# A feed-forward output layer with its weights stationary, 512 tokens moving, and results turned by VectorE

## The chip, the cores and the metric

The kernel runs on one core of one Trainium2 chip. The metric is the device time of one execution in microseconds, from the first to the last instruction with what the launch adds; the median of three runs counts. TensorE (PE in the profile) multiplies a stationary 128x128 operand, loaded by a weight load (PEld), with a moving operand of up to 512 columns and writes to PSUM, eight banks of 128 x 512 words. VectorE (DVE), ScalarE (ACT) and GpSimd (POOL) do the elementwise work, and SyncE (SP) issues nearly all DMAs.

## The reference

Three parts follow one another: a gated linear attention, a soft mixture of experts, and a feed-forward layer. The change is in the last; the weights of the second part's outputs (`c`) are built next to it.

```python
# x: 3072 tokens x 384 (batch 4, 768 each), 8 experts with 4 slots = 32 slots
logits = x @ phi                                   # 3072 x 32
d = softmax of logits over the tokens;  slot_input = d.T @ x
slot_out[e] = np.maximum(slot_input[e] @ w1[e], 0.0) @ w2[e]      # 32 x 384
c = softmax of logits over the slots               # 3072 x 32
x = c @ slot_out
# feed-forward: w_in 384 x 2048, w_out 2048 x 384
h = x @ w_in
g = np.maximum(0.01 * h, h)
return g @ w_out
```

## The kernel before, in words

All instructions are recorded with a cost and their dependences in a planner (class `Plan`), which sets the order on each engine by due times (`backward`, `forward`) and then emits the program. The code's order is thus only a wish; `plan.lead` makes operations due earlier. Buffers come from tags (`Tag`), each with a number of rotating buffers, and a buffer is taken in the order of the code: `t_w` has 33, `t_wi` 8, `t_x` and `t_q` and `t_qt` 5, `t_sc` and `t_yt` 4, `t_kt` and `t_cs` 2.

The program has three stages. **Attention** (0 to about 238 us) works on 12 units of 128 tokens; the last lines of a unit that matter here are the masking pass on VectorE (line 671), which the product of line 693 waits for. **Experts** (about 245 to 276 us) is a stream of 64 slabs of 384 KB of expert weights, loaded by SyncE as buffers come free; line 944 is the first expert layer, line 980 the second. The product of `slot_out` with `w_in` (lines 1024 to 1039) is made once, into `gs`, so that the first layer of the feed-forward part multiplies the weights `c` (32 slots, split in a high and a low part: 128 rows) with `gs`. **Feed-forward** (276 us to the end) is the stage of the change.

There, tokens are taken in `NB` = 8 blocks of `NG` = 384. `combine` makes the softmax over slots, for 18 of the 24 token tiles in one go ahead of the last attention unit's end and for the other six later. `combine_t` splits a block's weights in a high part (GpSimd, line 886) and a low part (VectorE, line 887), turns them on TensorE (line 891) and evicts them on ScalarE (line 894) to `cT[j]`. Six of the eight blocks are turned there, through the attention's PSUM bank `btr`, and the last two in the middle of the feed-forward stage.

`ffn1(j, f)` makes 128 of the 2048 hidden rows for block `j`: one matmul with 384 moving columns (line 1049), leaky ReLU on ScalarE (line 1051), rounded high part on ScalarE (line 1052), remainder on VectorE (line 1053). `ffn2(j, t, f)` adds 128 hidden rows into the result of token tile `t` of the block: the hidden values are stationary (128 hidden x 128 tokens) and the weights `woh`, `wol` (high and low part, 384 columns) move; three matmuls (lines 1066 to 1068) per step. After the 16th step ScalarE evicts the tile (line 1075) and SyncE stores it in rows of 1536 bytes (line 1076). Two blocks run side by side while the output weights are still converted (`conv_wo`: lines 445 to 449, 477 and 478); the other six follow one by one. The last block goes tile by tile.

## Time and profile before

| | us |
|---|---|
| median of three runs | 503.58 (503.57 to 504.87) |
| profiled execution, span | 503.0 |
| PE busy / DVE busy / ACT busy | 485.6 / 324.2 / 358.9 |
| 0 to 232 us: PE, DVE, ACT busy, DMA share | 219.69, 209.82, 211.45, 0.63 |
| 232 to 276 us | 42.45, 20.72, 13.87, 0.98 |
| 276 to 499.6 us | 223.50, 93.70, 133.15, 0.09 |
| 499.6 to 503 us | 0.00, 0.00, 0.48, 0.40 |

The profiled execution's span lies 0.6 us under the median of the runs. Busy times of engines overlap one another, and a matmul's printed length overlaps the next matmul's: what one costs in a row of matmuls is the distance between starts. A share is read stage by stage, since different engines and the DMA take turns in setting the pace.

### The profile page before, as it was taken

The numbers are of one execution on the slowest core, as the hardware profiler recorded it, in microseconds if no ns is written. First come the engines' busy times: TensorE is split into PE (matmuls) and PEld (weight loads), VectorE is DVE, ScalarE is ACT, GpSimd is POOL, SyncE is SP. The second block draws the span as 40 slices with busy tenths as digits, with TensorE's granted clock in tenths as the row PEclk, the third lists the DMA queues.
The fourth block names the chain that finished last, engine by engine and source line by source line (L and its number), as shares of the span: only waits on it lengthen the run. The fifth ranks groups of instructions, "written<-read, shape, count | busy, mean of one in ns | idle before, by whom it ended". The sixth has DMA issues, their size and how long they took to land.

```text
span 503.0 us, 10542 instructions
## 1 busy us (share of the span) xinstructions
PE 485.6 (97%) x4091; PEld 444.1 (88%) x4091; DVE 324.2 (64%) x686; ACT 358.9 (71%) x684; POOL 17.6 (3%) x37
## 2 busy tenths in 40 slices
PE   8797989999999999999999999999999999999997
PEld 8685879889989989888645999999999999999996
DVE  3778799999999999996544999324500552035300
ACT  6998999999999998955315999069801993079602
POOL 1010000001000100001000000000000000000000
PEclk9998999999999999999999999999999999999999
DMA  8877072473656596689999221011000010010002
GB/s 296 327 162 232 3 222 65 128 192 69 193 151 190 131 273 201 211 296 336 302 398 395 76 63 33 0 48 48 1 1 31 17 48 1 1 47 18 32 1 94
DMA packets 46890, 67.09 MB, mean 133 GB/s; under 512 B 22004, under 2 KB 28132, under 8 KB 46840
## 3 DMA queue, kind: packets, MB, share of 16 engines
q1 hardware_dynamic: 46088, 65.99, 41.1%
q8 instruction: 32, 0.52, 0.4%
q10 hardware_dynamic: 432, 0.39, 0.3%
q0 software_dynamic: 320, 0.03, 0.1%
q14 instruction: 18, 0.15, 0.1%
HBM read 61.59 MB, written 4.81 MB: 132 GB/s over the span
## 4 chain that ended last, share of the span: by engine, by line
PE 69%; ACT 14%; DVE 8%; DMA 7%; issue 1%; SPq 1%; DVEq 0%; ACTq 0%
PE b L1066 13%; PE b L1068 13%; PE b L1067 13%; PE bm L693 5%; PE bsc L668 5%; PE btr L653 4%; PE b L1049 4%; DMA w<-in_w_dram 4%; PE bc L571 3%; PE bsc L710 3%; ACT L186 3%; ACT qt L659 2%; DMA S<-in_w_dram 1%; DVE sc L671 1%; DMA w<-in_a_dram 1%
## 5 line engine op out<-in xcount | busy, mean ns | idle before, releaser
L1053 DVE TENSOR_TENSOR w<-x,w 128x384 fp32r<-128x384 f32 x128 | 69.0, 555 | 104.6 <-ACT w L1052 103.8
L1066 PE MATMUL b<-w 128*128 128x384 f32 x384 | 128.5, 335 | 0.0
L1068 PE MATMUL b<-w 128*128 128x384 f32 x384 | 128.3, 334 | 0.0
L1067 PE MATMUL b<-w 128*128 128x384 f32 x384 | 128.3, 334 | 0.0
L1066 PEld LDWEIGHTS b<-w 128*128 128x128 f32 x384 | 72.1, 188 | 0.3 <-ACT x L1051 0.2
L1067 PEld LDWEIGHTS b<-w 128*128 128x128 f32 x384 | 72.1, 188 | 0.0
L1068 PEld LDWEIGHTS b<-w 128*128 128x128 f32 x384 | 72.1, 188 | 0.0
L1075 ACT ACTIVATE k<-b 128x384 f32<-128x384 f32 x24 | 11.4, 488 | 79.1 <-PE b L1068 78.9
L1052 ACT ACTIVATE w<-x 128x384 fp32r<-128x384 f32 x128 | 63.5, 525 | 4.9 <-PE b L1068 3.2
L1051 ACT ACTIVATE x<-b 128x384 f32<-128x384 f32 x128 | 59.9, 487 | 2.5 <-PE b L1049 1.6
L668 PE MATMUL bsc<-qt,kt 96*128 96x128 f32 x384 | 51.1, 278 | 0.3 <-DVE kt L657 0.2
L668 PEld LDWEIGHTS bsc<-qt,kt 96*128 96x128 f32 x384 | 46.6, 192 | 1.9 <-DVE kt L657 0.5
L693 PE MATMUL bm<-sc,w 128*64 128x128 f32 (+1 forms) x384 | 35.5, 274 | 0.0
L671 DVE TENSOR_TENSOR sc<-bsc,tri_r 128x512 f32<-128x512 f32 x48 | 32.3, 683 | 3.1 <-PE bsc L668 2.7
L186 ACT ACT_TABLE_LOAD x25 | 32.1, 1283 | 2.6 <-issue 2.2
L653 PE MATMUL btr<-ident,q 128*96 128x128 f32 x192 | 30.0, 279 | 2.6 <-ACT qt L659 1.9
L693 PE MATMUL bm<-qt,S 96*48 96x128 f32 x320 | 31.1, 271 | 0.0
L653 PE MATMUL btr<-ident,k 128*96 128x128 f32 x192 | 29.6, 278 | 1.5 <-ACT kt L659 0.7
L710 PE MATMUL bsc<-w,k 128*96 128x48 f32 x320 | 29.8, 246 | 0.5 <-DVE sc L671 0.5
L710 PEld LDWEIGHTS bsc<-w,k 128*96 128x96 f32 x320 | 29.0, 165 | 1.1 <-DVE sc L671 0.7
L653 PEld LDWEIGHTS btr<-ident,q 128*96 128x96 f32 x192 | 20.9, 129 | 9.3 <-ACT qt L659 3.9
L659 ACT ACTIVATE qt<-btr 96x512 f32<-96x512 f32 x48 | 28.1, 589 | 1.1 <-PE btr L653 0.7
(183 smaller groups left out, 814.1 us busy)
## 6 DMA issues: line engine op xcount, KB each, us to landing
w<-in_w_dram SPq DMA_DIRECT2D x50, 384.0 KB
w<-in_qkv_dram SPq DMA_DIRECT2D x36, 384.0 KB
w<-in_a_dram SPq DMA_DIRECT2D x22, 384.0 KB
w<-in_wi_dram SPq DMA_DIRECT2D x16, 384.0 KB
w<-in_wo_dram SPq DMA_DIRECT2D x16, 384.0 KB
out_dram<-k SPq DMA_DIRECT2D x24, 192.0 KB
cs<-in_w_dram SPq DMA_DIRECT2D x4, 384.0 KB
k<-in_w_dram SPq DMA_DIRECT2D x6, 192.0 KB
```

Of the source, the lines that this page charges most:

```text
L186: self.preload(TABLES[name])
L653: T.transpose(b()[:96, P * i:P * i + P], src()[:, i].rearrange("p t d -> p (t d)"), ident)
L659: act(512, lambda b=b, t=t: A.activation(t()[:96], b()[:96, :].rearrange("p (i t) -> p i t", t=P), AF.Copy), [b], [t])
L668: T.matmul(b()[:, P * i:P * i + P], lhsT=k()[:96, i, :], rhs=q()[:96, i, :], start=True, stop=True)
L693: T.matmul(y()[64 * j:64 * j + m, o:o + P], lhsT=l, rhs=r, start=kind == 0, stop=kind == 1 or c == 0)
L710: T.matmul(b()[:96, D * i:D * i + D], lhsT=ks[i // 4]()[:, i % 4].rearrange("p t d -> p (t d)"), rhs=v()[:, D * g:D * g + D], start=True, ...
L1051: act(NG, lambda: A.activation(u(), b()[:, :NG], AF.Prelu, alpha=0.01), [b], [u])
L1052: act(NG, lambda: A.activation(g()[:, 0], u(), AF.Copy), [u], [(g, 0)])
L1053: dve(c_dve(NG), lambda: V.tensor_tensor(g()[:, 1], u(), g()[:, 0].bitcast(F32), op=ALU.subtract), [u, (g, 0)], [(g, 1)])
L1066: T.matmul(b()[:, :DM], lhsT=lh, rhs=wh()[:, i], start=f == FO[0], stop=False)
L1067: T.matmul(b()[:, :DM], lhsT=ll, rhs=wh()[:, i], start=False, stop=False)
L1068: T.matmul(b()[:, :DM], lhsT=lh, rhs=wl()[:, i], start=False, stop=f == FO[-1])
```

## The change

The block size `NG` goes from 384 to 512 tokens, so there are six blocks. A block is now 128 tokens of each of the four batch rows.

- `ffn2` of the first five blocks swaps the operands: the weights are stationary (every third column of `woh` or `wol`, a step of three words, for output columns 3m + k), and 512 tokens move. Three results per block (`k` = 0 to 2), each with 16 x 3 matmuls. A result has output columns on its partitions and tokens along its columns; VectorE turns it in blocks of 32 x 32 on the way out of PSUM, with a step of three words in the destination, into `of[j]` (tag `cs`). When all three are there, SyncE stores 16 pieces of 32 partitions x 4 x 96 words, rows of 384 bytes.
- the last block (`ffn2_last`) keeps the old form, 4 tiles with 384 columns of weights moving; its four tiles go step by step together, two are evicted by ScalarE and two by VectorE. It is held behind the last `ffn2` of the block before.
- `ffn1` works on 512 columns, with its high part in a `wi` buffer, the low part in a `w` buffer and the value before in an `sc` buffer.
- `combine` makes the softmax for 20 tiles in one go and for the last four later. `combine_t` is called block by block: two blocks after the expert layers are recorded, the third in the middle of the first two blocks, and each later one in the middle of the block before. It no longer uses the attention's PSUM bank.

```diff
--- before.py
+++ after.py
@@ -28,7 +28,7 @@
 G = 2 * H
 W = G * D
...
-NG = 3 * P
+NG = 4 * P
 NB = NT // NG
 NFC = DFF // P
 RND = 1.5 * 2.0 ** 23
@@ -860,38 +860,36 @@
 
     cT = {}
 
-    def combine(j0, j1, bank, after):
-
...
+        lgs = [("lg", c) for c in range(j0, j1)]
+        n = 4 * (j1 - j0) * NSL
+        t0 = slice(4 * j0, 4 * j1)
+        bc = lambda: rm()[:, t0].unsqueeze(2).to_broadcast([P, 4 * (j1 - j0), NSL])
+        key = (rm, j0)
+        lk = [("cw", j) for j in range(j0, j1)]
         dve(c_dve(n), lambda: V.tensor_reduce(rm()[:, t0], logits[:, t0], axis=AX.X, op=ALU.max), lgs, [key], after=after)
...
-        if j0 == 0:
-            combine_t(j0, j1, bank, lk)
-
-    def combine_t(j0, j1, bank, lk):
-        for j in range(j0, j1):
-            c4, b, t = (t_k if 4 <= j < 6 else t_kt)([P, 3, 4, NSL], F32R), bank(), slice(3 * j, 3 * j + 3)
-            ct = cT[j] = (t_q, t_yt)[j // 5]([P, NG], F32R)
-            w = lambda t=t: logits[:, t].unsqueeze(2).to_broadcast([P, 3, 2, NSL])
-            pool(c_pts(192), lambda c4=c4, w=w: GP.tensor_scalar(c4()[:, :, 0:2, :], w(), 1.0, 0.0, op0=ALU.mult, op1=ALU.add), [lk], [(c4, 0)])
-            dve(c_dve(192), lambda c4=c4, w=w: V.tensor_tensor(c4()[:, :, 2:4, :], w(), c4()[:, :, 0:2, :].bitcast(F32), op=ALU.subtract), [(c4, 0), lk], [(c4, 1)])
-
...
-            pe(0.33, tr, [(c4, 0), (c4, 1)], [b], after=[phi_mm] if 4 <= j < 6 else [])
-            act(384, lambda ct=ct, b=b: A.activation(ct(), b()[:, :NG], AF.Copy), [b], [ct])
+        dve(c_dve(n), lambda: V.tensor_tensor(logits[:, t0], logits[:, t0], bc(), op=ALU.mult), [key], lk)
+
+    def combine_t(j):
+        c4, b, t = t_kt([P, 4, 4, NSL], F32R), bank(), slice(4 * j, 4 * j + 4)
+        ct = cT[j] = (t_yt if j < 4 else t_qt if j < 5 else t_kt)([P, NG], F32R)
+        w = lambda: logits[:, t].unsqueeze(2).to_broadcast([P, 4, 2, NSL])
+        lk = ("cw", j)
+        pool(c_pts(256), lambda: GP.tensor_scalar(c4()[:, :, 0:2, :], w(), 1.0, 0.0, op0=ALU.mult, op1=ALU.add), [lk], [(c4, 0)])
+        dve(c_dve(256), lambda: V.tensor_tensor(c4()[:, :, 2:4, :], w(), c4()[:, :, 0:2, :].bitcast(F32), op=ALU.subtract), [(c4, 0), lk], [(c4, 1)])
+
+        def tr():
+            for k in range(4):
+                T.transpose(b()[:, P * k:P * k + P], c4()[:, k].bitcast(F32).rearrange("p r s -> p (r s)"), ident)
+
+        pe(0.44, tr, [(c4, 0), (c4, 1)], [b])
+        act(NG, lambda: A.activation(ct(), b()[:, :NG], AF.Copy), [b], [ct])
 
 
     psb = Area(tc, "psb", after=(psa,), space=PSUM)
@@ -900,7 +898,7 @@
     t_rm = Tag(mem, "rm", [P, NTILE], 1)
     rm = t_rm()
     plan.lead = 30.0
-    combine(0, 6, b_tr, ())
+    combine(0, NB - 1, ())
     plan.lead = 0.0
     rd, siT, wb = t_sm([P, 1]), t_dd([P, 3, NSL]), t_kt([P, 4, NSL])
     dg, mt = t_kt([P, P]), t_sm()
@@ -1046,33 +1044,67 @@
     def ffn1(j, f):
         b = bank()
         w, o = gs[f // 4], P * (f % 4)
-        pe(0.17, lambda: T.matmul(b()[:, :NG], lhsT=w()[:, o:o + P], rhs=cT[j](), start=True, stop=True), [(w, o // 256), cT[j]], [b])
-        u, g = t_x(), t_w([P, 2, NG], F32R)
+        pe(0.227, lambda: T.matmul(b()[:, :NG], lhsT=w()[:, o:o + P], rhs=cT[j](), start=True, stop=True), [(w, o // 256), cT[j]], [b])
+        u, gh, gl = t_sc(), t_wi([P, NG], F32R), t_w([P, NG], F32R)
         act(NG, lambda: A.activation(u(), b()[:, :NG], AF.Prelu, alpha=0.01), [b], [u])
-        act(NG, lambda: A.activation(g()[:, 0], u(), AF.Copy), [u], [(g, 0)])
-        dve(c_dve(NG), lambda: V.tensor_tensor(g()[:, 1], u(), g()[:, 0].bitcast(F32), op=ALU.subtract), [u, (g, 0)], [(g, 1)])
-        hl[j, f] = g
-
-    ob = {}
-
-    def ffn2(j, t, f):
+        act(NG, lambda: A.activation(gh(), u(), AF.Copy), [u], [gh])
+        dve(c_dve(NG), lambda: V.tensor_tensor(gl(), u(), gh().bitcast(F32), op=ALU.subtract), [u, gh], [gl])
+        hl[j, f] = gh, gl
+
+    ob, of, outs = {}, {}, []
+
+    def ffn2(j, k, f):
+
+        if f == FO[0]:
+            ob[j, k] = bank()
+            if k == 0:
+                of[j] = t_cs([P, NG // 32, 32, 3])
+        b, (gh, gl), o = ob[j, k], hl[j, f], of[j]
+        wh, wl, i = woh[f // 2], wol[f // 2], f % 2
+
+        def mmul():
+            h, l = (w()[:, i].rearrange("p (m k) -> p m k", k=3)[:, :, k] for w in (wh, wl))
+            T.matmul(b()[:, :NG], lhsT=h, rhs=gh(), start=f == FO[0], stop=False)
+            T.matmul(b()[:, :NG], lhsT=h, rhs=gl(), start=False, stop=False)
+            T.matmul(b()[:, :NG], lhsT=l, rhs=gh(), start=False, stop=f == FO[-1])
+
+        op = pe(0.68, mmul, [gh, gl, (wh, i), (wl, i)], [b])
+        if f == FO[-1]:
+            outs.append(op)
+            dve(c_dve(NG) + 0.1, lambda: V.transpose(o()[:, :, :, k], b()[:, :NG].rearrange("p (n t) -> p n t", t=32)), [b], [(o, k)])
+            if k == 2:
+                for a in range(4):
+                    for bi in range(B):
+                        r0 = S * bi + P * j
+
+                        def store(a=a, bi=bi, r0=r0):
+                            SY.dma_start(
+                                out[r0:r0 + P, 96 * a:96 * a + 96].rearrange("(n t) d -> t n d", t=32),
+                                o()[32 * a:32 * a + 32, 4 * bi:4 * bi + 4].rearrange("p n d k -> p n (d k)"),
+                            )
+
+                        plan.add("SP", 0, store, [(o, k) for k in range(3)], [], nbytes=P * 96 * 4)
+
+    def ffn2_last(j, t, f):
         if f == FO[0]:
             ob[j, t] = bank()
-        b, g = ob[j, t], hl[j, f]
+        b, (gh, gl) = ob[j, t], hl[j, f]
         wh, wl, i = woh[f // 2], wol[f // 2], f % 2
 
         def mmul():
-            lh, ll = g()[:, 0, P * t:P * t + P], g()[:, 1, P * t:P * t + P]
+            lh, ll = gh()[:, P * t:P * t + P], gl()[:, P * t:P * t + P]
             T.matmul(b()[:, :DM], lhsT=lh, rhs=wh()[:, i], start=f == FO[0], stop=False)
             T.matmul(b()[:, :DM], lhsT=ll, rhs=wh()[:, i], start=False, stop=False)
             T.matmul(b()[:, :DM], lhsT=lh, rhs=wl()[:, i], start=False, stop=f == FO[-1])
 
-        pe(0.515, mmul, [(g, 0), (g, 1), (wh, i), (wl, i)], [b])
+        pe(0.52, mmul, [gh, gl, (wh, i), (wl, i)], [b], after=[outs[-1]])
         if f == FO[-1]:
             o = t_k()
-            c, bi = divmod(3 * j + t, B)
-            r0 = S * bi + P * c
-            act(384, lambda: A.activation(o(), b()[:, :DM], AF.Copy), [b], [o])
+            r0 = S * t + P * j
+            if t % 2:
+                act(384, lambda: A.activation(o(), b()[:, :DM], AF.Copy), [b], [o])
+            else:
+                dve(c_dve(384), lambda: V.tensor_copy(o(), b()[:, :DM]), [b], [o])
             plan.add("SP", 0, lambda: SY.dma_start(out[r0:r0 + P, :], o()), [o], [], nbytes=P * DM * 4)
 
     load_slabs(LATE[0])
@@ -1092,7 +1124,9 @@
     layer2(1)
     output(0)
     output(1)
-    combine(6, NB, bank, [si])
+    combine(NB - 1, NB, [si])
+    combine_t(0)
+    combine_t(1)
     plan.lead = 25.0
     product()
     for f in FO[:4]:
@@ -1110,19 +1144,21 @@
             if i + ahead < NFC:
                 ffn1(j, FO[i + ahead])
         for j in range(2):
-            for t in range(3):
-                ffn2(j, t, f)
+            for k in range(3):
+                ffn2(j, k, f)
+        if i == NFC // 2:
+            combine_t(2)
     for j in range(2, NB):
-        if j == 3:
-            combine_t(6, NB, bank, ("cw", 6))
-        for f in FO:
+        for i, f in enumerate(FO):
             ffn1(j, f)
             if j < NB - 1:
-                for t in range(3):
-                    ffn2(j, t, f)
-    for t in range(3):
-        for f in FO:
-            ffn2(NB - 1, t, f)
+                for k in range(3):
+                    ffn2(j, k, f)
+            else:
+                for t in range(B):
+                    ffn2_last(j, t, f)
+            if i == NFC // 2 and j < NB - 1:
+                combine_t(j + 1)
     plan.emit()
     for a in (mem, psb, dram):
         a.close()
```

The order that the planner makes of it, at the places that the steps of the prediction rest on. First VectorE at the end of attention, before: `logits` and `rm` are the softmax over slots, `sc<-bsc,tri_r` is the masking pass.

```order
L671 TENSOR_TENSOR sc<-bsc,tri_r 128x512
L875 TENSOR_SCALAR rm<-rm 128x18
L876 RECIPROCAL rm<-rm 128x18
L877 TENSOR_TENSOR logits<-logits,rm 128x576
L671 TENSOR_TENSOR sc<-bsc,tri_r 128x512
L887 TENSOR_TENSOR k<-logits,k 128x3x64 x2
L887 TENSOR_TENSOR kt<-logits,kt 128x3x64
L448 SCALAR_TENSOR_TENSOR w<-w 128x384
L657 COPY kt<-btr 96x512
L671 TENSOR_TENSOR sc<-bsc,tri_r 128x512
L449 SCALAR_TENSOR_TENSOR wi<-w 128x384
L887 TENSOR_TENSOR kt<-logits,kt 128x3x64
```

After, up to the last masking pass and the reduction that follows it:

```order
L449 SCALAR_TENSOR_TENSOR wi<-w 128x384
L671 TENSOR_TENSOR sc<-bsc,tri_r 128x512
L874 TENSOR_REDUCE rm<-logits 128x20
L657 COPY kt<-btr 96x512
L671 TENSOR_TENSOR sc<-bsc,tri_r 128x512
L875 TENSOR_SCALAR rm<-rm 128x20
L876 RECIPROCAL rm<-rm 128x20
L877 TENSOR_TENSOR logits<-logits,rm 128x640
L671 TENSOR_TENSOR sc<-bsc,tri_r 128x512
L759 TENSOR_REDUCE mx<-bsc 128x1
```

The subtractions of line 887 are no longer among the masking passes; the softmax passes are 640 wide instead of 576.

Second, TensorE in the middle of a block, before. The first name behind the arrow is the moving operand, the second the stationary one; numbers tell buffers apart.

```order
L1049 MATMUL b_4922<-q_3438,qt_3922 128x384
L1066 MATMUL b_4814<-w_4060,w_4850 128x384
L1067 MATMUL b_4814<-w_4060,w_4850 128x384
L1068 MATMUL b_4814<-w_4070,w_4850 128x384
L1066 MATMUL b_4821<-w_4060,w_4850 128x384
L1067 MATMUL b_4821<-w_4060,w_4850 128x384
L1068 MATMUL b_4821<-w_4070,w_4850 128x384
```

After, in the fourth block:

```order
L1047 MATMUL b_5021<-yt_4676,qt_3884 128x512
L1067 MATMUL b_4879<-wi_5006,w_4201 128x512
L1068 MATMUL b_4879<-w_5011,w_4201 128x512
L1069 MATMUL b_4879<-wi_5006,w_4213 128x512
L1067 MATMUL b_4885<-wi_5006,w_4201 128x512
L1068 MATMUL b_4885<-w_5011,w_4201 128x512
L1069 MATMUL b_4885<-wi_5006,w_4213 128x512
```

Per 128 hidden rows of a block it is ten matmuls as before (a third group of three isn't shown), each 512 wide, for 512 tokens instead of 384; the hidden values (`wi`, `w`) now move and the output weights stand.

Third, TensorE where the second and third block meet, after. `b_3944` and its two neighbours are results of the first block, `b_3952`, `b_3967` and `b_3980` of the second, `b_4545` of the third.

```order
L1069 MATMUL b_3944<-wi_4509,w_4400 128x512
L1047 MATMUL b_4601<-yt_4270,qt_3878 128x512
L1067 MATMUL b_3952<-wi_4522,w_4393 128x512
L1068 MATMUL b_3952<-w_4527,w_4393 128x512
L1069 MATMUL b_3952<-wi_4522,w_4400 128x512
L1047 MATMUL b_4609<-yt_4270,qt_3888 128x512
L1047 MATMUL b_4616<-yt_4270,qt_3884 128x512
L1047 MATMUL b_4618<-yt_4270,qt_3888 128x512
L1067 MATMUL b_3967<-wi_4522,w_4393 128x512
L1068 MATMUL b_3967<-w_4527,w_4393 128x512
L1069 MATMUL b_3967<-wi_4522,w_4400 128x512
L1047 MATMUL b_4631<-yt_4270,qt_3884 128x512
```

The first-layer matmuls of the third block stand in a bunch between the second block's last groups, and the last group of `b_3980` stands far later, among the fourth block's last.

## Rows read from the trace of the kernel before

**Rows 1.** Busy us (instructions) by stretch: PE, PEld, DVE, ACT, POOL; PEclk, DMA, GB/s
```profile
232.00:252.00 20.00, 19.38 (x275) 14.47 (x275) 10.44 (x40) 6.57 (x18) 1.00 (x3) 1.00 0.92 311
252.00:272.00 20.00, 19.07 (x232) 8.70 (x228) 6.34 (x33) 4.17 (x8) 0.99 (x2) 1.00 1.03 400
...
280.00:499.00 219.00, 219.00 (x1268) 218.89 (x1267) 89.96 (x187) 129.24 (x298) 0.00 (x0) 1.00 0.09 28
```

**Rows 2.** Timeline of TensorE, output layer: start, length, line, operation, operands, count
```profile
329.79 0.33 PE L1066 MATMUL b<-w 128*128 128x384 f32 x1
...
330.83 0.33 PE L1066 MATMUL b<-w 128*128 128x384 f32 x1
```

**Rows 3.** Timeline, matmuls of 256 columns of lines 1032 and 1033, and what follows
```profile
275.78 0.28 PE L1032 MATMUL b<-w,sc 128*128 128x256 f32 x1
...
276.73 1.04 PE L1049 MATMUL b<-q,qt 128*128 128x384 f32 x5
```

**Rows 4.** Timeline, line 571: 512 and 256 columns in turn; merged lengths
```profile
121.95 0.74 PE L571 MATMUL bc<-w,tri_r 128*128 128x512 f32 x3
...
122.18 0.52 PE L571 MATMUL bc<-w,tri_r 128*128 128x256 f32 x2
...
122.30 0.40 PE L571 MATMUL bc<-w,tri_r 128*128 128x512 f32 x1
```

**Rows 5.** Groups by line and form: operands, count, busy us, mean ns, idle before
```profile
L448 DVE SCALAR_TENSOR_TENSOR w<-w 128x384 int32<-128x384 int32 x32 | 17.3, 550 | 0.1
...
L478 DVE TENSOR_TENSOR w<-w 128x384 fp32r<-128x384 f32 x16 | 8.8, 552 | 0.1
```

**Rows 6.** Timeline of TensorE, weight loads of 128 columns with 32 columns moving
```profile
243.37 0.93 PE L923 MATMUL bm<-kt,acc 128*128 128x32 f32 x6
244.13 0.42 PE L832 MATMUL bc<-ident 128*128 128x128 f32 x2
```

**Rows 7.** Timeline of VectorE at the end of attention
```profile
224.86 0.75 DVE L872 TENSOR_TENSOR logits<-logits,rm 128x576 f32<-128x576 f32 x1
...
229.73 0.92 DVE L887 TENSOR_TENSOR k<-logits,k 128x192 fp32r<-128x192 f32 x2
...
230.84 0.55 DVE L448 SCALAR_TENSOR_TENSOR w<-w 128x384 int32<-128x384 int32 x1
...
232.97 0.34 DVE L887 TENSOR_TENSOR kt<-logits,kt 128x192 fp32r<-128x192 f32 x1
233.24 0.68 DVE L671 TENSOR_TENSOR sc<-bsc,tri_r 128x512 f32<-128x512 f32 x1
```

**Rows 8.** Timeline of TensorE between the last attention product and the expert layer
```profile
237.51 0.87 PE L891 MATMUL btr<-ident,kt 128*128 128x128 f32 x6
238.22 0.55 PE L735 MATMUL bm<-ident,yt 112*128 112x112 f32 x4
...
244.85 1.50 PE L944 MATMUL b<-w,dd 128*32 128x256 f32 x24 [0.30 <-DVE dd L925]
```

**Rows 9.** The chain of work that ended last: start, length, what
```profile
260.67 7.81 DMA w<-in_w_dram
268.52 1.49 PE b L980 x10
```

**Rows 10.** Timeline of VectorE at the start of the feed-forward stage
```profile
277.06 0.56 DVE L1053 TENSOR_TENSOR w<-x,w 128x384 fp32r<-128x384 f32 x1
```

**Rows 11.** Groups of the whole program, columns as in rows 5
```profile
L1052 ACT ACTIVATE w<-x 128x384 fp32r<-128x384 f32 x128 | 63.5, 525 | 4.9 <-PE b L1068 3.2
L1051 ACT ACTIVATE x<-b 128x384 f32<-128x384 f32 x128 | 59.9, 487 | 2.5 <-PE b L1049 1.6
...
L659 ACT ACTIVATE qt<-btr 96x512 f32<-96x512 f32 x48 | 28.1, 589 | 1.1 <-PE btr L653 0.7
```

**Rows 12.** Timeline at the end of the program
```profile
499.59 0.49 ACT L1075 ACTIVATE k<-b 128x384 f32<-128x384 f32 x1 [0.60 <-PE b L1068]
500.11 0.33 SPq L1076 DMA_DIRECT2D out_dram<-k  x1
```

More of the change, by code (lines that the diff above doesn't have):

```diff
@@ L861, in tile_kernel, with combine @@
     cT = {}
-    def combine(j0, j1, bank, after):
-        i0, i1 = 3 * j0, 3 * j1
-        lgs = [("lg", c) for c in range(i0 // 4, (i1 + 3) // 4)]
-        n = (i1 - i0) * NSL
-        t0 = slice(i0, i1)
-        bc = lambda: rm()[:, t0].unsqueeze(2).to_broadcast([P, i1 - i0, NSL])
-        key, lk = (rm, j0), ("cw", j0)
+    def combine(j0, j1, after):
+        lgs = [("lg", c) for c in range(j0, j1)]
[4 more added lines that the diff above has]
+        lk = [("cw", j) for j in range(j0, j1)]
@@ L871, in combine @@
         dve(c_dve(n), lambda: V.tensor_reduce(rm()[:, t0], logits[:, t0], axis=AX.X, op=ALU.max), lgs, [key], after=after)
-        dve(c_dve(n), lambda: V.tensor_tensor(logits[:, t0], logits[:, t0], bc(), op=ALU.subtract), lgs + [key], [lk])
-        act(n, lambda: A.activation(logits[:, t0], logits[:, t0], AF.Exp), [], [lk], table="E")
-        dve(c_dve(n), lambda: V.tensor_reduce(rm()[:, t0], logits[:, t0], axis=AX.X, op=ALU.add), [lk], [key])
+        dve(c_dve(n), lambda: V.tensor_tensor(logits[:, t0], logits[:, t0], bc(), op=ALU.subtract), lgs + [key], lk)
@@ L875, in combine @@
+        act(n, lambda: A.activation(logits[:, t0], logits[:, t0], AF.Exp), [], lk, table="E")
+        dve(c_dve(n), lambda: V.tensor_reduce(rm()[:, t0], logits[:, t0], axis=AX.X, op=ALU.add), lk, [key])
         dve(0.1, lambda: V.tensor_scalar(rm()[:, t0], rm()[:, t0], 1e-9, None, op0=ALU.add), [], [key])
         dve(0.25, lambda: V.reciprocal(rm()[:, t0], rm()[:, t0]), [], [key])
-        dve(c_dve(n), lambda: V.tensor_tensor(logits[:, t0], logits[:, t0], bc(), op=ALU.mult), [key], [lk])
-        if j0 == 0:
-            combine_t(j0, j1, bank, lk)
@@ L881, in combine_t @@
-    def combine_t(j0, j1, bank, lk):
-        for j in range(j0, j1):
-            c4, b, t = (t_k if 4 <= j < 6 else t_kt)([P, 3, 4, NSL], F32R), bank(), slice(3 * j, 3 * j + 3)
-            ct = cT[j] = (t_q, t_yt)[j // 5]([P, NG], F32R)
-            w = lambda t=t: logits[:, t].unsqueeze(2).to_broadcast([P, 3, 2, NSL])
-            pool(c_pts(192), lambda c4=c4, w=w: GP.tensor_scalar(c4()[:, :, 0:2, :], w(), 1.0, 0.0, op0=ALU.mult, op1=ALU.add), [lk], [(c4, 0)])
-            dve(c_dve(192), lambda c4=c4, w=w: V.tensor_tensor(c4()[:, :, 2:4, :], w(), c4()[:, :, 0:2, :].bitcast(F32), op=ALU.subtract), [(c4, 0), lk], [(c4, 1)])
-            def tr(c4=c4, b=b):
-                for k in range(3):
-                    T.transpose(b()[:, P * k:P * k + P], c4()[:, k].bitcast(F32).rearrange("p r s -> p (r s)"), ident)
-            pe(0.33, tr, [(c4, 0), (c4, 1)], [b], after=[phi_mm] if 4 <= j < 6 else [])
-            act(384, lambda ct=ct, b=b: A.activation(ct(), b()[:, :NG], AF.Copy), [b], [ct])
+        dve(c_dve(n), lambda: V.tensor_tensor(logits[:, t0], logits[:, t0], bc(), op=ALU.mult), [key], lk)
```

## The prediction

> **What bounds the kernel now.** [...] In a single stretch of its timeline the starts say what one matmul costs: seven starts from 329.79 to 330.83 are six steps, 1.04 / 6 = 0.1733 us for 384 columns [rows 2]. The printed length of 0.33 us is pipeline depth and overlaps the next. So the stage is 1280 such steps (1152 of the output layer, 128 of the first layer), 221.8 us, and the six transposes of line 891 that lie in it.
>
> Then the chain of work before that stage: its last long links are DMA loads of expert weights, the last one 7.81 us from 260.67, and TensorE goes on at 268.52 when it lands [rows 9]. In 252 to 272 us the DMA engines are full (1.03, 400 GB/s); in 232 to 252 they are at 0.92 [rows 1]. What comes before 232 us therefore matters as far as it lets loads start earlier.
>
> **What the change does to the matmuls.** The columns that stream are the same: 1280 x 384 = 491,520 before; after, 96 + 720 matmuls of 512 and 192 of 384 (the last block keeps the old form) are 417,792 + 73,728 = 491,520. What falls is the number of matmuls, from 1280 to 1008. A gain comes only from what a matmul costs beyond its columns. Two clean runs, each matmul with its own weights, give that: 256 columns take 0.95 / 8 = 0.1188 us (eight steps from 275.78 to 276.73, [rows 3]), 384 take 0.1733 [rows 2]. A line through both puts 512 at 0.1733 + 0.0545 = **0.2278 us**. The sum: 816 x 0.2278 + 192 x 0.1733 = 185.9 + 33.3 = 219.2, against 221.8: **-2.6 us**. Both ends: the last digit of the times allows 0.120 at 256, so 0.2266 at 512 and -3.6; the trace also has 512-column matmuls of this type, in the cumulative sums of line 571, and there the step from 121.95 to 122.18 is 0.23 and the pair of 512 and 256 is 0.35 [rows 4], which with 0.1188 leaves 0.231 and at the rounding's end 0.235: 816 x 0.0072 = +5.9 on top. I take the line, since those sums run in threes with waits for their operands between them, and the runs of 256 and 384 don't.
>
> Ten more 128-column transposes than before lie in this stage (16 against 6, since four of the six combine blocks are now turned inside it): six of them take 238.22 - 237.51 = 0.71 us [rows 8], so 0.118 each and **+1.2 us**.
>
> **What the new stationary operand costs.** The weights are read with a step of three words (12 bytes), every third column of a row. No row has such a weight load. Below: nothing, if it takes no longer than a contiguous one; no reason lets it gain. How long a contiguous one takes is seen where little streams: six loads of 128x128 with 32 columns each start at 243.37 and the next group at 244.13, 0.76 / 6 = 0.127 us [rows 6]. It hides under 0.2278 until it is 1.8 times as long. Above: at twice, 0.254 us would be the step, 720 x 0.026 = +19 us. The nearest strided row is VectorE's read of every second word (8 bytes) at line 448: 550 ns against 552 for the contiguous line 478 [rows 5]. I take nothing.
>
> [...]
>
> **What feeds TensorE.** ScalarE's two passes over a first-layer tile grow from 487 + 525 ns to about 0.59 + 0.7: 512 columns out of PSUM take 589 [rows 11], and 525 x 512 / 384 = 700 is an estimate for the second. That is 1.3 us for each 10 matmuls or 2.28 us, so ScalarE has room, and it no longer evicts results of five blocks. The 24 evictions move to 15 turns on VectorE. No row shows one; from below it is like the 512-wide eviction, 0.59, from above I take twice that. Three per block of some 36 us cover themselves, except at the four block changes where the next block wants their banks. There the order of the program keeps one finished group of a block back as spare work. Price: 0 to 4 x 1.2 = 4.8 us; I take **+0.3**, near nothing, since the stage before has practically no gap with the same scheme [rows 1]. The first ScalarE-VectorE chain of the stage, which ends with a VectorE pass of 0.56 at 277.06 [rows 10], is longer by some 0.4 us, but TensorE does its five first-layer matmuls from 276.73 [rows 3] meanwhile, and they are longer too (5 x 0.0545): **+0.1**. Four combine blocks' ScalarE and VectorE work now also lies in this stage, under cover of VectorE's idle 129 us of 219.
>
> Stores: 80 of 48 KB in 384-byte rows take the place of 20. SyncE issues one in about 0.33 us (the last one starts at 500.11, [rows 12]); 16 per block are 5 us of 36, and three times as much would hide as well. The tail is the same: eviction at 499.59, store at 500.11, end at 503.0, 3.4 us [rows 12]. The last tile is now evicted by VectorE instead of ScalarE: **+0.05**.
>
> **What moves ahead of the stage.** Before, four VectorE subtractions of line 887 stand in front of the last masking pass of line 671 at 233.24, on which the last attention product waits: 229.73 to 230.84 is 1.11 us for three, 232.97 to 233.24 is 0.27 for the fourth [rows 7]. They are gone from there. Four passes over 576 logits become 640, each 0.75 us [rows 7], an estimate of a ninth of that, 0.08 each: +0.3. So that stretch shortens by 1.1 us. Behind it six transposes go, 0.71 us [rows 8], and the start of the expert layer at 244.85 could come up to 1.8 us earlier. Only what the DMA engines have idle can be had from it: 0.08 x 20 us = 1.6 us in 232 to 252 [rows 1]. Ends: -1.6 and, if the queue is paced by its bytes and the new load order is no better, 0 (or a little above, 0.3). I take **-0.9**. The transposes of the first two combine blocks move in between the second expert layer's matmuls, ahead of the last eight, which wait for the load that lands at 268.5 anyway.
>
> **Sum.** -2.6 + 1.2 + 0.3 + 0.1 + 0.05 - 0.9 = -1.85 us. The profiled execution's span is 503.0 us and the median of the runs 503.58; I take the 0.6 us between them as unchanged and set the change against the median: **501.7 us**, 0.4% faster.
>
> **Rivals.**
> 1. *Everything good together*: 512 columns at 0.2266 and the DMA gap wholly used, 501.7 - 1.0 - 0.7 = 500.0, without gaps 499.6. For it: equal extra cost per matmul at 256 and 384. Against: rows 4.
> 2. *The stepped weight load sets the pace* (slower than before). Place: each of 720 output-layer matmuls; it decides from 1.8 times the contiguous load on. At 1.8 nothing, at 1.9 (0.241) +9.7 us or 511, at twice 520.6. For it: no row shows a 12-byte step, and a 512-column moving stream reads SBUF beside it. Against: the 8-byte row [rows 5], and a third more (0.169) would still hide.
> 3. *A 512-column matmul costs what line 571 shows*, 0.231 to 0.235: +2.6 to +5.9, so 504.3 to 507.6, with 505.5 (0.2325) in the middle. For it: the same type and width [rows 4]. Against: waits in those sums, no such extra at 384.
> 4. *Nothing to be had in front and gaps at the block changes*: front 0, gaps 1.5: 501.7 + 0.9 + 1.2 = 503.8, no change. For it: a full DMA queue from 252 on [rows 1].
>
> **How the numbers follow.** Forecast (500.3 to 503.2) 0.46; rival 1 (499.0 to 500.3) 0.10; rival 4 (503.2 to 504.6) 0.19; rival 3 (504.3 to 507.6) 0.11; rival 2 (above 506) 0.14. A measurement of this kernel tells 0.3%, 1.5 us, from no change. Faster than 502.1: two thirds of the forecast and rival 1, 0.42; slower than 505.1: rival 2 and most of rival 3, 0.24; within: 0.34. The range from 499.0 to 506.0 leaves out rival 2 and half of rival 3, about 0.2.
>
> **What would show it.** After: steps of 0.227 to 0.229 us between starts of 512-column matmuls, of both layers alike. If the output layer's step is above the first layer's, the stepped load costs; if both are near 0.233, rival 3 holds. TensorE's sum over the stage should be near 220 us without idle time, the last expert load should land 0.5 to 1.5 us before 268.5, and the last matmul should start some 3.8 us before the end. Idle time of TensorE behind the VectorE turns, or a last store that is late, would make the forecast wrong.

## The result and the profile after

The changed kernel takes 507.19 us (median of five runs, 506.36 to 510.57) against 503.58 before: ratio 1.0073, 95% interval 1.0047 to 1.0099. It is slower by 0.7%, where 501.7 was forecast, and outside the range. Its profiled execution has a span of 506.7 us, 3.76 more than before (502.99 to 506.75).

Busy times by stretch, columns as in [rows 1]:

```profile
232.00:252.00 20.00, 19.03 (x280) 13.55 (x282) 9.73 (x43) 4.46 (x13) 0.00 (x0) 1.00 0.95 333
280.00:499.00 219.00, 218.67 (x982) 212.28 (x981) 98.09 (x169) 115.45 (x211) 1.26 (x2) 1.00 0.12 28
```

The stage is still all TensorE, at a granted clock of 1.00: 982 instructions in 219 us against 1268 before. The DMA engines work a little more in 232 to 252 us (0.95 against 0.92). So what a matmul costs has to be read. TensorE's timeline in the output layer, to be held against [rows 2]:

```profile
329.58 0.39 PE L1067 MATMUL b<-wi,w 128*128 128x512 f32 x1
329.81 0.40 PE L1068 MATMUL b<-w 128*128 128x512 f32 x1
...
330.99 0.39 PE L1067 MATMUL b<-wi,w 128*128 128x512 f32 x1
```

Six steps from 329.58 to 330.99 are 1.41 us: **0.235 us** for a matmul, where the forecast had 0.2278. Over the whole stage nearly all 512-column steps lie between 0.229 and 0.241, 0.2346 on average: 0.2348 behind a matmul of the output layer, 0.2324 behind one of the first layer (L1047). The last block, in the old form, still steps by 0.1735. Groups of weight loads by line in 280 to 499 us (count, busy us, mean ns):

```profile
L1068 PEld LDWEIGHTS b<-w 128*128 128x128 f32 x235 | 59.4, 253 | 0.0
...
L1047 PEld LDWEIGHTS b<-yt,qt 128*128 128x128 f32 x58 | 10.8, 187 | 2.3 <-ACT sc L1049 0.9 <-DVE cs L1074 0.2
```

The stepped load is recorded 65 ns longer than the contiguous one of the first layer. It is printed 253 ns long, but steps of 0.235 us go past it.

The span's 3.76 us, by TensorE's starts in the two traces: the first first-layer matmul 275.58 to 273.93 (-1.65); from there to the first output-layer matmul 2.07 to 2.38 (+0.31); from that to the start of the last 221.51 to 226.34 (**+4.83**); from there to the end 3.82 to 4.10 (+0.28).

Of the other parts: the groups of the stage's VectorE and ScalarE work, and the chain of work around the one long gap of TensorE (its starts at 436.45 and 437.18):

```profile
L1074 DVE STREAM_TRANSPOSE cs<-b 128x512 f32<-128x512 f32 x15 | 12.4, 863 | 31.1 <-PE b L1069 30.9
L1050 ACT ACTIVATE wi<-sc 128x512 fp32r<-128x512 f32 x95 | 59.0, 640 | 30.1 <-PE b L1069 24.1 <-PE b L1098 4.9
L1049 ACT ACTIVATE sc<-b 128x512 f32<-128x512 f32 x95 | 54.6, 606 | 61.3 <-PE b L1047 38.4 <-DVE w L1051 22.6
```

```profile
433.24 1.67 DMA out_dram<-cs
434.90 0.86 DVE cs L1074
...
436.02 0.62 ACT wi L1050
436.64 0.49 ACT sc L1049
...
437.18 0.50 PE b L1047
```

A turn on VectorE takes 0.863 us, inside its bounds of 0.59 and 1.2. At this block change it waits for stores out of the buffer that it fills; ScalarE and the first layer queue up behind it, and TensorE loses 0.5 us. At the front, TensorE's timeline has the last eight expert matmuls (two records each) 1.71 us ahead of [rows 9], behind eight of the moved transposes. TensorE comes to these straight from other expert matmuls (start 264.38), without the wait for a load that the prediction put them into, so they take their 1.0 us of its time (265.79 to 266.81). At the end, VectorE's copy of the last tile stands beside [rows 12]:

```profile
264.38 1.47 PE L978 MATMUL b<-w,h 128*32 128x384 f32 x16
265.79 1.09 PE L889 MATMUL b<-ident,kt 128*128 128x128 f32 x8
266.81 1.50 PE L978 MATMUL b<-w,h 128*32 128x384 f32 x16
```

```profile
503.02 0.56 DVE L1107 COPY k<-b 128x384 f32<-128x384 f32 x1 [0.49 <-PE b L1098]
```

The miss is in the 816 steps of 512 columns. Three causes were open: the width itself (the forecast's rival 3), the stepped weights (in another form than rival 2, since 0.235 is no doubled load), or the ScalarE and VectorE work beside the matmuls.

### The profile page after: what moved, and what is told of

It reads as the page before. It is cut to its first block, busy times and chain, and to the rows that moved or that the text cites. A ratio compares the mean times of both kernels' runs of the same rounds, so it can differ in the third digit from the quotient of the medians.

```text
span 506.7 us, 9835 instructions
## 1 busy us (share of the span) xinstructions
PE 487.7 (96%) x3819; PEld 440.3 (87%) x3819; DVE 334.4 (66%) x669; ACT 346.0 (68%) x596; POOL 17.3 (3%) x35
## 4 chain that ended last, share of the span: by engine, by line
PE 62%; ACT 20%; DMA 8%; DVE 7%; issue 2%; SPq 0%; ACTq 0%; DVEq 0%
PE b L1069 11%; PE b L1068 11%; PE b L1067 11%; PE b L1047 4%; ACT L186 4%; PE bm L693 3%; PE btr L653 2%; PE bc L571 2%; PE bsc L668 2%; PE b L1098 2%; ACT qt L659 2%; PE b L1097 2%; PE b L1096 2%; PE b L942 2%; PE b L978 2%
## 5 line engine op out<-in xcount | busy, mean ns | idle before, releaser
L1051 DVE TENSOR_TENSOR w<-sc,wi 128x512 fp32r<-128x512 f32 x96 | 64.8, 688 | 77.8 <-ACT wi L1050 77.4
L1049 ACT ACTIVATE sc<-b 128x512 f32<-128x512 f32 x96 | 55.2, 606 | 61.4 <-PE b L1047 38.4
L1067 PE MATMUL b<-wi,w 128*128 128x512 f32 x240 | 95.5, 398 | 0.0
L1068 PE MATMUL b<-w 128*128 128x512 f32 x240 | 95.5, 398 | 0.0
L1069 PE MATMUL b<-wi,w 128*128 128x512 f32 x240 | 95.3, 397 | 0.0
L1050 ACT ACTIVATE wi<-sc 128x512 fp32r<-128x512 f32 x96 | 59.6, 640 | 30.1 <-PE b L1069 24.1
L1067 PEld LDWEIGHTS b<-wi,w 128*128 128x128 f32 x240 | 60.6, 252 | 2.1
L1068 PEld LDWEIGHTS b<-w 128*128 128x128 f32 x240 | 60.6, 253 | 0.0
L1069 PEld LDWEIGHTS b<-wi,w 128*128 128x128 f32 x240 | 60.5, 252 | 0.0
L1074 DVE STREAM_TRANSPOSE cs<-b 128x512 f32<-128x512 f32 x15 | 12.4, 863 | 31.1 <-PE b L1069 30.9
```

What stands on the lines that cost most here:

```text
L1049: act(NG, lambda: A.activation(u(), b()[:, :NG], AF.Prelu, alpha=0.01), [b], [u])
L1050: act(NG, lambda: A.activation(gh(), u(), AF.Copy), [u], [gh])
L1051: dve(c_dve(NG), lambda: V.tensor_tensor(gl(), u(), gh().bitcast(F32), op=ALU.subtract), [u, gh], [gl])
L1067: T.matmul(b()[:, :NG], lhsT=h, rhs=gh(), start=f == FO[0], stop=False)
L1068: T.matmul(b()[:, :NG], lhsT=h, rhs=gl(), start=False, stop=False)
L1069: T.matmul(b()[:, :NG], lhsT=l, rhs=gh(), start=False, stop=f == FO[-1])
```

## Experiments

Ratios are to the kernel before on the same chip; on the three chips it took 504.24, 504.20 and 503.86 us. A step in us is the distance between the starts of two matmuls; a step in words is the distance at which the columns of a weight operand are read. "Stage" is from the start of the first output-layer matmul to that of the last, in the profiled execution; 221.51 before, 226.34 after.

**1. Matmuls by themselves (m1_widths).** Behind the program's end:

```diff
+        for q in range(25):
+            T.matmul(d[q % 4][:, :512], lhsT=wc(q), rhs=g[:, :512], start=True, stop=True)
+        for q in range(25):
+            T.matmul(d[q % 4][:, :512], lhsT=w3(q), rhs=g[:, :512], start=True, stop=True)
...
```

> The changed kernel with matmuls appended behind its end (some 90 us more, their results unused): 25 in a row for each case, each with its own weights, nothing else running: 256, 384, 448, 480, 508 and 512 moving columns with contiguous weights; 512 with weights at a step of three and of two words, 384 and 256 at a step of three; 512 columns accumulated into one bank; 512 columns with the same weights each time. Then 512 columns beside ScalarE passes, beside VectorE passes, and with stepped weights beside both. Width theory: the 512-column case with contiguous weights already steps at 0.2325 to 0.2355 us, as the output layer of the changed kernel does, and the stepped one the same. Stepped-load theory: contiguous 0.2266 to 0.2290, stepped 0.2335 or more, and with 384 columns the stepped load shows fully, at 0.19 or more against 0.1733. Company theory (ScalarE and VectorE beside it slow the matmul): both near 0.228 when alone, 0.233 or more beside passes of the others.

Measured: TensorE's timeline, one row for each case of 25. The cost of one is the distance to the next row's start divided by 25. L1185 is 512 columns with contiguous weights, L1195 the same added up in one bank, L1197 the same with one weight operand loaded again each time. L1187 has a step of three words, L1189 of two; L1191 and L1193 are 384 and 256 columns at a step of three; L1209 and L1212 are contiguous 512 beside ScalarE and beside VectorE, L1215 stepped beside both in turn.

```profile
526.87 5.85 PE L1185 MATMUL b<-wi,w 128*128 128x512 f32 x25
532.57 6.04 PE L1187 MATMUL b<-wi,w 128*128 128x512 f32 x25
538.45 5.99 PE L1189 MATMUL b<-wi,w 128*128 128x512 f32 x25
544.28 4.60 PE L1191 MATMUL b<-wi,w 128*128 128x384 f32 x25
548.72 4.49 PE L1193 MATMUL b<-wi,w 128*128 128x256 f32 x25
553.04 5.86 PE L1195 MATMUL b<-wi,w 128*128 128x512 f32 x25
558.75 5.83 PE L1197 MATMUL b<-wi,w 128*128 128x512 f32 x25
564.41 0.39 PE L1201 MATMUL b<-wi,w 128*128 128x512 f32 x1
564.64 5.83 PE L1209 MATMUL b<-wi,w 128*128 128x512 f32 x25
570.31 0.39 PE L1216 MATMUL b<-wi,w 128*128 128x512 f32 x1
...
576.90 6.05 PE L1215 MATMUL b<-wi,w 128*128 128x512 f32 x25
```

Contiguous 512: (532.57 - 526.87) / 25 = 0.228; the first few steps are longer, then they settle at 0.2267, the forecast's lower end. A step of three: 5.88 / 25 = **0.2352**, the changed kernel's own figure; of two: 0.2332. Beside ScalarE it is 0.2268 and beside VectorE 0.2268, so company costs nothing here, and stepped beside both it is (6.05 - 0.39) / 24 = 0.2358. The width and company theories fall. But the stepped-load theory's number for 384 falls too: 4.44 / 25 = 0.1776, not 0.19. And 256 columns, with 4.32 / 25 = 0.173 against 0.12, show what the load takes when it sets the pace: some 1.5 times the contiguous one (experiment 4). It fits under 0.2267 with 0.05 to spare, and costs 0.0085 there all the same.

**2. The same change with contiguous weights (e_contig).** The two passes that write the output weights store every third column together; the stationary operand and the copies of the last block follow.

```diff
-        act(HW, lambda: A.activation(wh()[:, h], tmp()[:, 1], AF.Copy), [(tmp, 1)], [(wh, h)])
+        kt = lambda: tmp()[:, 1].rearrange("p (m k) -> p k m", k=3)
+        km = lambda w: w()[:, h].rearrange("p (k m) -> p k m", k=3)
+        act(HW, lambda: A.activation(km(wh), kt(), AF.Copy), [(tmp, 1)], [(wh, h)])
...
-            h, l = (w()[:, i].rearrange("p (m k) -> p m k", k=3)[:, :, k] for w in (wh, wl))
+            h, l = (w()[:, i, P * k:P * k + P] for w in (wh, wl))
```

> The changed kernel with one thing different: the output layer's weights are stored with every third column together, so that the stationary operand of each output-layer matmul is contiguous. 720 matmuls are touched. Width theory: step stays 0.2345, time 506.5 to 507.8, ratio to the kernel before 1.006 to 1.009. Stepped-load theory: weight loads go from 252 to 188 ns in the records and the step to 0.228, 720 x 0.0067 = 4.8 us less, 502.4 us, ratio 0.998.

Measured: 504.00 us, ratio 0.999 (0.9971 to 1.0009). The stage falls from 226.34 to 222.20. Weight loads of the output layer, and TensorE's timeline there:

```profile
L1070 PEld LDWEIGHTS b<-w 128*128 128x128 f32 x240 | 45.1, 188 | 9.5
```

```profile
329.66 0.39 PE L1069 MATMUL b<-wi,w 128*128 128x512 f32 x1
...
331.02 0.39 PE L1069 MATMUL b<-wi,w 128*128 128x512 f32 x1
```

Six steps in 1.36 us, 0.2267; the first layer's steps fall to 0.2286 on average as well, though their own weights were contiguous all along. The stepped weights are the cause: without them the stage is 4.1 us shorter. The forecast of 502.4 for this theory was set against 503.58; as a ratio, 0.998, it lies inside the measured interval. The stage gave back less than the 4.8 us of the forecast, because its gaps grew: 27 steps are longer than 0.26, together 3.1 us above 0.23 (16 steps and 1.7 us above 0.235 in the changed kernel, one step and 0.1 before), most of them around first-layer matmuls that wait for ScalarE's pass over a PSUM bank. What grew lies in the first 50 us of the stage, 10 such steps with 1.3 us against 2 with 0.2, where the output weights are still converted. There the two passes that bring every third column together now read with a step of three words. ScalarE's, in the changed kernel and in this one (270 to 325 us):

```profile
L477 ACT ACTIVATE w<-w 128x384 fp32r<-128x384 f32 x15 | 7.9, 528 | 0.1
...
L479 ACT ACTIVATE w<-w 128x384 fp32r<-128x384 f32 x15 | 11.3, 752 | 0.5 <-DVE w L449 0.4
```

It takes 752 ns instead of 528, and VectorE's 674 instead of 551. The new layout is thus paid in part by the passes that write it; that these passes make the gaps is argued from the place, not shown by a run of its own.

**3. The front alone (e_front), and the swap at the old width (e_swap384).** e_front keeps the old matmuls and moves the transposes: out of the first combine, two blocks between the expert layers, six into the stage.

```diff
-        if j0 == 0:
-            combine_t(j0, j1, bank, lk)
...
     combine(6, NB, bank, [si])
+    combine_t(0, 2, bank, ("cw", 0))
...
+            if i == NFC // 2 and j < NB - 1:
+                combine_t(j + 1, j + 2, bank, ("cw", 0 if j + 1 < 6 else 6))
```

> The kernel before with only the other part of the change: 384-token blocks and tokens stationary as before, but the combine blocks are turned late (two between the expert layers, six inside the feed-forward stage), so that the end of the attention is free of them. If the front part of the change is worth 1.7 us by itself and twelve more transposes inside the stage cost 0.118 each (1.4 us): 503.2, ratio 0.999 to 1.000. If the front gain needs the larger blocks: 505.0. If transposes inside the stage are hidden: 501.9.

Measured: 503.38 us, ratio 0.998 (0.9959 to 1.0001); first first-layer matmul at 274.33 (-1.25), stage 222.88 (+1.37 for twelve transposes, 0.114 each). As its first case had it: in the trace, what the front gains, the stage gives back.

e_swap384 adds the swapped output layer with NG at 384, so that the moving operand is 384 wide:

```diff
-            T.matmul(b()[:, :DM], lhsT=lh, rhs=wh()[:, i], start=f == FO[0], stop=False)
+            T.matmul(b()[:, :NG], lhsT=h, rhs=g()[:, 0], start=f == FO[0], stop=False)
...
```

> The kernel of e_front with the swap of operands added at the old width: weights stationary (step of three words), 384 tokens moving in seven of eight blocks, results turned by VectorE and stored in 384-byte rows. 1008 matmuls are touched. Width theory: their step stays 0.1735 and the time that of e_front within 0.6 us. Stepped-load theory: the load is 64 ns longer than a contiguous one; with the 0.127 us of a bare contiguous load that is 0.191, above 0.1735, so 1008 x 0.0175 = 17.6 us more, some 521 us; if the recorded 252 ns were its pace, 580 us.

Measured: 513.31 us, ratio 1.0183 (1.0151 to 1.0215); stage 227.56, 4.68 more than e_front. Over 1008 matmuls that is 0.0046 each; the steps by themselves cost 0.1776 - 0.1735 = 0.0041. Both forecasts were off: it isn't free, and a load of 0.191 isn't the pace. By experiment 4 this load takes 0.175, level with a 384-column matmul, so a part of the 0.0041 may be the load itself. The rest of the time is no matter of the matmuls. The end of the program on VectorE and in SyncE's queue:

```profile
504.28 0.69 DVE L1072 STREAM_TRANSPOSE cs<-b 128x384 f32<-128x384 f32 x1 [0.36 <-PE b L1068]
505.00 5.55 SPq L1080 DMA_DIRECT2D out_dram<-cs  x12
```

Here a swapped block came last in the order, and its twelve short-row stores take 5.55 us after the last turn: the tail is 8.98 us instead of 3.82.

**4. What a stepped load costs, by step and width (m2_steps, m3_grid).** Cases as in 1, other widths and steps.

```diff
+    def ws(s):
+        return lambda q: woh[q % 8]().rearrange("p i n -> p (i n)").rearrange("p (m k) -> p m k", k=s)[:, :P, (q // 8) % s]
...
+            T.matmul(d[q % 4][:, :256], lhsT=ws(4)(q), rhs=g[:, :256], start=True, stop=True)
...
```

> The changed kernel with 20 cases of 25 matmuls appended (about 100 us more, their results unused): 64, 256, 384 and 512 moving columns, each with 128x128 weights at a step of 1, 2, 3, 4 and 6 words. Load-length theory (a stepped load takes longer and is otherwise hidden): at 64 columns the step is the bare load, about 0.12 contiguous and 0.17 at three words, and at 384 and 512 all five are alike. Contention theory (each stepped load also takes some reads from the moving stream, whether or not it is hidden): 512 columns cost 0.2335 to 0.2355 at steps of two and three, 384 cost 0.177 at three. [...]

Measured, read as in 1: L1186, L1188, L1190, L1192 are 256 columns at steps of 2, 3, 4, 6 words, L1206 to L1212 the same at 512.

```profile
529.92 3.16 PE L1186 MATMUL b<-wi,w 128*128 128x256 f32 x25
532.92 4.53 PE L1188 MATMUL b<-wi,w 128*128 128x256 f32 x25
537.29 6.00 PE L1190 MATMUL b<-wi,w 128*128 128x256 f32 x25
543.13 5.86 PE L1192 MATMUL b<-wi,w 128*128 128x256 f32 x25
548.83 4.50 PE L1194 MATMUL b<-wi,w 128*128 128x384 f32 x25
...
579.24 6.00 PE L1206 MATMUL b<-wi,w 128*128 128x512 f32 x25
585.07 6.04 PE L1208 MATMUL b<-wi,w 128*128 128x512 f32 x25
590.96 6.04 PE L1210 MATMUL b<-wi,w 128*128 128x512 f32 x25
596.83 6.08 PE L1212 MATMUL b<-wi,w 128*128 128x512 f32 x25
```

At 256 columns: 0.120 at two words, as contiguous; 0.175 at three, 0.234 at four, 0.228 at six. The contiguous load and that of two words set the pace where only 64 columns move (L1174 and L1176; the granted clock is 1.00 there, see the last section):

```profile
502.84 2.84 PE L1174 MATMUL b<-wi,w 128*128 128x64 f32 x24
505.51 2.40 PE L1176 MATMUL b<-wi,w 128*128 128x64 f32 x19
507.28 0.64 PE L1176 MATMUL b<-wi,w 128*128 128x64 f32 x4
```

(505.51 - 502.84) / 24 = 0.111 contiguous, (507.28 - 505.51) / 15 = 0.118 at two words (the third row holds the last four of the second's 19). So a load at two words takes a few ns longer than a contiguous one, at three words some 1.5 times as long, at four and six about twice. The load-length theory holds there; why the load takes longer with the step isn't shown.

At 512 columns it is 0.2332 at two words, 0.2356 at three, 0.2348 at four, 0.2371 at six, against 0.2267. At four and six words the load by itself (0.234 and 0.228 by the rows at 256 columns) is longer than 0.2267, so it isn't covered. At two and three words it is, with 0.11 and 0.05 us to spare, and the matmul gets 6.6 and 8.9 ns longer all the same. That much of the contention theory holds.

> The changed kernel with 24 cases of 25 matmuls appended (some 130 us more, their results unused): 384, 416, 432, 448, 464, 480, 496 and 512 moving columns, each with weights at a step of one, two and three words. The load is hidden at all of these widths at a step of one and two (bare 0.118 us and less) and at three (0.174) from 400 columns or so. If what a stepped load takes from a hidden matmul belongs to full-width 512 alone: two words cost nothing more up to 496. If it grows with the width: a few ns at 416, 6 to 9 at 496. If it is tied to the remainder of the width: no order in it.

Measured, mean step in ns of 25 matmuls (from the starts; the contiguous 512 once settled):

```
columns       384    416    432    448    464    480    496    512
contiguous  173.3  186.8  195.9  202.7  210.0  216.7  223.3  226.7
two words   173.3  186.7  193.3  203.5  211.7  216.7  225.5  233.3
three words 177.1  193.4  196.6  204.4  213.3  219.8  224.5  235.1
```

The line through 256 and 384 columns gives 186.7 at 416, 200.0 at 448, 220.0 at 496 and 226.7 at 512. Contiguous weights lie on it at 384, 416 and 512, and some 3 ns above it from 432 to 496. What a step of two or three words adds, -2.6 to 8.4 ns, has no order in the width. So the price isn't a full bank's alone (three words cost 6.6 ns at 416), nor does it grow steadily with the width (two words cost nothing at 480); the third case fits best, and why stays open. One caution: m1_widths had 448 contiguous columns as well, at 0.206 where this table has 0.2027, and 508 columns at 0.228, more than 512. From 432 to 508 columns a case can thus be 4 ns off from one run to another, and most differences there are smaller. At 512 the three runs agree within 1 ns.

**5. Can the front's gain be kept? (e_mid, e_early4, e_contig_early)** All three turn more of the combine blocks among the expert matmuls: e_mid all eight blocks of the old form, with priority; e_early4 four of the eight, just ahead of the last eight expert matmuls; e_contig_early four of the six of e_contig.

```diff
+    combine(NB - 1, NB, [si])
+    plan.lead = 25.0
+    for j in range(4):
+        combine_t(j)
+    plan.lead = 0.0
     layer2(0)
     layer2(1)
...
```

> The kernel before (384-token blocks, tokens stationary, all matmuls as they were) with all 24 transposes of the combine blocks moved out of the end of the attention and into the gaps of the second expert layer, none in the feed-forward stage. If the front is worth 1.3 to 1.7 us here as in the changed kernel and e_front, and the six transposes that leave the stage another 0.65: 501.2 to 501.7 on a chip where before takes 503.6, ratio 0.9955. If the new place gives back what the front gains: 0.999 to 1.000.

> The kernel before (384-token blocks, tokens stationary) with four of the eight combine blocks turned just ahead of the last expert matmuls and four inside the feed-forward stage. Against e_front six transposes leave the stage, 6 x 0.109 = 0.65 us. If the twelve fit into the wait for the last expert load: ratio 0.9965 to 0.997, as good as e_contig_early, and then the swap of operands, even with contiguous weights, is worth nothing by itself. If they delay the expert layer as in e_mid: 1.000 or more.

> The changed kernel with contiguous output weights (as in e_contig) and four of the six combine blocks turned in the gaps of the second expert layer, before the feed-forward stage (8 transposes left in it instead of 16). If the transposes that leave the stage cost their 0.109 each there and nothing in the new place: 0.9 us below e_contig, so a ratio to before of 0.997 (502.2 to 503.4 us). If the new place delays the last expert matmuls by as much: 0.999, no change against e_contig.

> The kernel of e_contig_early once more, beside e_early4 on one chip: ratio to before 0.9945 to 0.999 if its gain of 0.3% is real; 1.000 or more if it was this chip's scatter.

> The changed kernel once more, beside the others on one chip. Every theory: ratio to before 1.005 to 1.010, stage from the first output-layer matmul to the last 226.3 us.

Measured: e_mid 505.78 us, ratio 1.0046 (1.0025 to 1.0068), slower. e_early4 504.33, 1.0006 (0.9988 to 1.0024), no change. e_contig_early 502.54, 0.9968 (0.9945 to 0.9991), and again 501.70, 0.9962 (0.9943 to 0.9982): faster than both kernels. The changed kernel again 506.97, 1.0068 (1.0042 to 1.0093), stage 226.35. The stages came as expected: 221.07 in e_mid, 222.20 in e_early4 (0.68 less than e_front), 221.15 and 221.37 in e_contig_early. In e_mid the front gave it back. TensorE at the start of its second expert layer, and the chain of work there:

```profile
255.88 0.66 PE L953 MATMUL b<-ident,kt 128*128 128x128 f32 x4 [1.36 <-DVE kt L949]
256.70 0.55 PE L889 MATMUL b<-ident,kt 128*128 128x128 f32 x3 [0.16 <-DVE kt L885]
257.43 0.55 PE L889 MATMUL b<-ident,kt 128*128 128x128 f32 x3 [0.18 <-DVE kt L885]
```

```profile
263.87 0.81 PE b L889 x6
264.68 6.66 PE b L978 x80
```

Transposes that wait for VectorE stand ahead of the expert matmuls, the first of these starts at 257.91 (256.58 in e_front), and the first first-layer matmul is late, at 276.91. In e_early4 the expert layers start at 241.00 and the first first-layer matmul still comes at 273.95: its last six transposes start at 266.01, after a wait for VectorE's split of the weights. The start of the expert layers differs between executions of one program: 242.85 to 243.64 in five of the changed kernel (m1_widths, m2_steps and m3_grid begin with it), with the first first-layer matmul at 273.58 to 274.71; 241.70 and 239.42 in the two of e_contig_early. So gains of the front below 1 us can't be read from one trace.

The time of e_contig_early came out as forecast, but not by the forecast's account. From the first expert matmul to the first first-layer matmul it takes 31.89 and 31.88 us, against 30.89 in e_contig: the eight transposes cost in their new place the 1.0 us that they save in the stage. Its gain lies ahead of that, in expert layers that start earlier than e_contig's (242.53); why they do stays open. Nor does it speak for the swap, although it beats e_early4: from the first first-layer matmul to the end it takes 227.84 and 228.05 us, e_early4 in the old form 228.09, the kernel before 227.41.

## Why the prediction failed

**The weights (the failed step).** "It hides under 0.2278 until it is 1.8 times as long ... I take nothing." The load is some 1.5 times as long (0.175 by the row at 256 columns, against a contiguous one of 0.111, where [rows 6] had given 0.127) and does hide; the matmul that it hides under gets longer nevertheless, 0.2267 to 0.2352 alone and 0.2346 on average in the kernel. The error was to price a covered load by its length only. Its upper end, +19 us by a doubled load, an assumption that no row showed, has the right cause and the wrong mechanism; so has rival 2 as it was put, which allowed nothing below 1.8. The row of line 448 (a stepped read on VectorE, [rows 5]) said nothing on a read beside a moving stream.

**The width.** The line through 256 and 384 columns gave 0.2278 with a lower end of 0.2266; contiguous 512 measures 0.2267. That step held. The first 512-column matmuls of a case are slower, however: in m1_widths the case behind the stepped ones begins like this, and one that has settled looks like that (parts of L1195 and L1197):

```profile
553.04 2.24 PE L1195 MATMUL b<-wi,w 128*128 128x512 f32 x9
...
561.92 1.30 PE L1197 MATMUL b<-wi,w 128*128 128x512 f32 x5
```

(2.24 - 0.39) / 8 = 0.231 against (1.30 - 0.39) / 4 = 0.2275. So the reading of line 571 [rows 4] as 0.231 to 0.235, rival 3's price, may be that of matmuls which alternate in width and never settle; that is argued, not shown. Rival 3 came out near the measured time with the wrong cause.

**The sign that was to tell them apart.** "If the output layer's step is above the first layer's, the stepped load costs; if both are near 0.233, rival 3 holds." Both lie about 0.233, and it was the stepped load. On average the output layer's step is above the first layer's, 0.2348 against 0.2324, in both traces of the changed kernel, so the sign leaned the right way; but the first layer's step was itself above 0.2267. During a first-layer matmul the next one's stepped load may run, and the effect may outlast it; that is argued. Only the contiguous version (experiment 2) told.

**The terms.** Matmuls: 816 x (0.2346 - 0.2278) = 5.5 us above the term of -2.6. That is nearly the whole miss: 5.6 us by the spans (3.76 + 1.85), 5.5 by the medians. The other terms come to +0.8: transposes in the stage +0.9 for 1.2 (before 6 in 0.49 us, after 16 in 1.43); gaps 1.7 us for 0.3, of which 0.8 at the block changes, the turn that waited for stores among them (the place named but the price too low), and the rest behind the transposes and at first-layer matmuls in mid-block, places that the sum did not have; start of the stage +0.31 for 0.1, from longer passes in a chain that nothing covers; tail +0.28 for 0.05, of which VectorE's copy explains 0.07; front -1.65 in the first profile and -0.87 to -2.00 in the other four executions of the same program, for -0.9 with the DMA's idle share (-1.6) as its bound, and although eight transposes did not fall into a wait. (The two sums differ by 0.7: the six first-layer matmuls ahead of the stage are in both the first term and the start, 0.3, and the rest is the rounding of the steps.) The turns on VectorE (0.863) and ScalarE's passes (0.606 and 0.640, for 0.59 and 0.7) were sized right.

**What a right sum would have been.** With 0.2352 from experiment 1 in its place: -2.6 + 816 x 0.0074 = +3.4, and with the other terms as forecast 507.8, against 507.19. That it comes so near is partly luck, since the misses of the gaps and of the front go opposite ways.

## What to carry to other kernels

A weight load that is hidden wasn't free here when it was stepped by three words (0.2352 us for a 512-column matmul against 0.2267): store the stationary operands so that each is contiguous, and count what that costs in the pass that writes them; here the stage took back 4.1 us of 226, with ScalarE's pass grown from 528 to 752 ns. Swapping operands to stream more columns per matmul could gain here only what a matmul costs beyond its columns, an estimated 13 ns (the line through 0.1733 at 384 and 0.2267 at 512 columns, followed to none), no more than its longer passes, gaps and tail cost: with contiguous weights it ended where the old form with the same front was (0.999 and 0.998). Work moved out of a full stage must find a real wait in its new place: here the transposes took as much of TensorE's time there as they left behind (1.0 us for eight, e_contig_early), or more where matmuls stood behind them (e_mid, the first first-layer matmul at 276.91 against 275.58).
